# DeltaNet attention and a gelu layer on one core: row steps of the second group's inverse between decoding operations, early key norms, a back turn as copies, and U and Y out in three copies

## The chip, the cores and the metric

The kernel runs on one core of one Trainium2 chip. The metric is device time in microseconds of that core. The kernel before takes 661.88 us, the median of three runs (660.78 to 662.9). The profile is that of one execution of 660.83 us, whose recorded span is 659.1 us.

## What is computed

Attention with a state that is updated at every token, and then a two-layer network on what it gives. B = 4 batches, H = 8 heads, S = 768 tokens, D = 48; the network is 384 to 2048 to 384 wide, for 3072 tokens.

```python
k_n = k / (np.linalg.norm(k, axis=-1, keepdims=True) + 1e-06)
state = np.zeros((B, H, D, D))
for t in range(S):
    y[:, :, t] = einsum('bhd,bhde->bhe', q[:, :, t], state)
    v_old = einsum('bhde,bhd->bhe', state, k_n[:, :, t])
    state += beta[:, :, t] * einsum('bhd,bhe->bhde', k_n[:, :, t], v[:, :, t] - v_old)
x = y.transpose(0, 2, 1, 3).reshape(B * S, H * D)
h = x @ w_in
out = (0.5 * h * (1 + erf(h / sqrt(2)))) @ w_out
```

q, k, v and beta arrive as 32-bit floats, w_in and w_out as 64-bit floats, which the kernel itself turns into 32-bit ones.

## The kernel before

**Tiling.** The 768 tokens of each head are cut into 12 chunks of 64. A chunk has two *units* (a = 0, 1), each with two batches, one on each half of the 128 partitions, times 8 heads. Two chunks make a *group*: chunks 0 and 1 are group 0, chunks 2 and 3 group 1. Within a chunk the recurrence is solved at once: U is the solution of a triangular system of 64 by 64 for each head and batch, whose inverse depends on keys and beta alone and so can be made ahead; the state St passes from chunk to chunk. Q, K and V of a unit are tiles with a row for each token.

**The inverse of a group.** `grams` (L375) takes the keys' products on PE (`products`, L363) and copies them out on ACT: off-diagonal blocks to G (L382), diagonal blocks of 32 to `diag` (L386 and, for the lower half, L389). `prep` (L296), `root` (L317) and `factors` (L265) make the norms and the factor of each row; `scales` (L429) spreads the factors into XM, and `flip` (L436) turns the diagonal blocks by a DVE transpose into Nu, where the systems lie along the partitions, and scales them. Then come 30 row steps, `eliminate(j)` (L441): a product into tmp (L446) and a sum into Nu (L448), each of which reads what the one before it wrote. `back` (L454) turns Nu back by three DVE transposes: x = 0 into XM (L457), x = 1 into the right half of Zf, x = 2 into its left half (both L461). `clear` (L465) zeroes the lower left block of Zf; in group 0 one of its four parts is an ACT operation (L471), the others POOL memsets (L473). Last, `join` in group 0 (L481; `join_run`, L519, in later groups) computes the block that couples the two 32-blocks: products psJ, times a factor into XM on DVE (L503), products psJ again, copies into Zf on ACT (L507).

**A chunk.** `against_state` (L591) multiplies keys and queries by the state, `subtract` (L612) makes the right-hand side W and keeps the queries' part as y, `solve` (L628) multiplies by the inverse into psU and copies it out as U: four ACT copies of 64 partitions x 192 for each unit (L643), since pairs of heads lie on exchanged partition halves in PSUM. `use` (L645) gives psY = P U, where P are the masked products of queries and keys (`queries`, L393, copied out at L403, masked at L409), and the state's addition psS; `next_state` (L667) adds that to St on DVE, `read` (L671) takes psY out as x, again in four operations (ACT copies in chunks 0 and 1, L676; DVE additions of y later, L678). `turn` (L686) transposes x through psX into xT (L700).

**The network.** For chunks 0 and 1, `fc1` (L717) has 16 parts f of 128 of the 2048 columns (psH, L723; gelu into G by ACT, L725), and `fc2` (L732) gathers psO over the 16 f (L736). From chunk 2 on, `first_layer` and `second_layer` do the second layer with seven products of half size in place of eight (psX, psY, psZ, L761). `fc1` of chunk 1 begins before chunk 0's second layer is done: its first EARLY = 8 parts (L711) are put between chunk 0's last `fc2` steps (L847).

**The weights.** The 64-bit weights come in 16 parts: 0 to 7 are w_in, 8 to 15 w_out, each good for two f (`fetch`, L199). A part is decoded by `begin` (exponent field, DVE, L218), `exponents` (ACT, L223), `mantissas` (DVE, L230 and L232) and `signed` (DVE, L237 and L238), each operation on 128x768. That makes five DVE operations and one ACT operation for each part.

**Norms of chunks 2 and 3.** `sum_of_squares` (L285) has ACT square the keys of one head and sum them along the row, 16 calls for each chunk. V of these chunks is scaled by the norms on ACT, one call for each head (`scale_head`, L330).

**What sets the order.** The *head*, from the loads to chunk 0's xT and the decoding of parts 0 to 2, is written out by hand on all engines (L871 to L956): each engine runs its instructions in the order in which the program issues them. After it comes `plan` (L973 to L1044): steps with a time each, in units of some 58 us; all are issued in the order of their times (`emit`, L858). DVE then runs them in that order (L1045). On the other engines a scheduler may still move them; `keep_in_program_order` holds single ACT operations in place, and `together` (L563) a run of PE matmuls. `late` (L962) gives back the pools of the start, among them the PSUM tiles and the staging buffers, and zeroes Kb. An instruction waits in its engine's queue for the semaphores of its inputs, and what is behind it waits too.

Of the kernel before, what the change touches and what calls it, by code (L numbers as in the profile page):

```python
# [16 lines left out]
def kernel(  # L17
# [160 lines left out]
    G = cpool.tile([128, NF, NA * 128], F32)  # L178
    St = cpool.tile([128, NA, 2, NP, D], F32)
# [41 lines left out]
    def exponents(n):  # L221
        e = halves[n][3]
        i = nc.scalar.activation(e, e, ACT.Relu, bias=lim[:, 0:1], scale=float(2 ** 23))  # L223
        if n in (3, 4):
            tc.keep_in_program_order(i)

    def mantissas(n):
        dst, lo, hi, e = halves[n]
        bits = dst.bitcast(U32)
        nc.vector.tensor_scalar(bits, hi, 0xFFFFF, 0x100000, op0=ALU.bitwise_and,  # L230
                                op1=ALU.bitwise_or)
        nc.vector.scalar_tensor_tensor(dst, lo, 2.0 ** -32, bits, ALU.mult, ALU.add)  # L232

    def signed(n):

        dst, lo, hi, e = halves.pop(n)
        nc.vector.scalar_tensor_tensor(e, hi, 0x80000000, e, ALU.bitwise_and, ALU.bitwise_or)  # L237
        nc.vector.scalar_tensor_tensor(dst, dst, 2.0 ** -20, e.bitcast(F32), ALU.mult, ALU.mult)  # L238
        after = n + (NS if n < n_in else len(slots))
        if (after < n_in) == (n < n_in):  # L240
            fetch(after)

    def decode_steps(first, last):
        def start_(n):
            begin(n)
            exponents(n)

        steps = [(0.6, start_, first), (1.5, mantissas, first)]
        for n in range(first, last):
            if n + 1 < last:  # L250
                steps += [(0.6, start_, n + 1), (1.9, signed, n), (1.5, mantissas, n + 1)]
        return steps + [(1.9, signed, last - 1)]
# [20 lines left out]
    def squares(u, n, engine=None):  # L273
# [5 lines left out]
        if engine is None:  # L279
            nc.scalar.activation(ksq, kd, ACT.Square)  # L280
        else:
            engine.tensor_tensor(ksq, kd, kd, op=ALU.mult)
        nc.vector.tensor_reduce(n, ksq, axis=AX.X, op=ALU.add)  # L283

    def sum_of_squares(u, h):  # L285

        if "both" not in ns:
            n23 = wk.tile([128, 2 * NA, H], F32, tag="n0", name="n0", bufs=1)
            ns[2], ns[3] = n23[:, 0:NA], n23[:, NA:]
            ns["both"] = n23  # L290
        if h == 0:
            u.ksq = wk.tile([128, H, D], F32, tag="ksq", name="ksq")
        tc.keep_in_program_order(nc.scalar.activation(
            u.ksq[:, h], u.Kn[:, h, 0:D], ACT.Square, accum_out=ns[u.c][:, u.a, h:h + 1]))
# [35 lines left out]
    def scale_head(u, h):  # L330
        tc.keep_in_program_order(
            nc.scalar.mul(u.V[:, h], u.V[:, h], ns[u.c][:, u.a, h:h + 1]))
# [42 lines left out]
    def grams(us):  # L375
# [7 lines left out]
        if g > 0:  # L383
# [3 lines left out]
            for p in range(2):  # L387
                lower = slice(p * C + HB, (p + 1) * C)
                put("gram", Ds[g][lower, span], Gs[g][lower, span])  # L389

    Ps = {}
# [33 lines left out]

    def eliminate_steps(g):
# [14 lines left out]
        def eliminate(j):  # L441
# [3 lines left out]
            tmp = tmp[:, 0:n * j].rearrange("q (i c) -> q i c", i=n)  # L445
            nc.vector.tensor_tensor(tmp, nu[:, j + 1:, j:j + 1].to_broadcast([128, n, j]),  # L446
                                    nu[:, j:j + 1, 0:j].to_broadcast([128, n, j]), op=ALU.mult)
            nc.vector.tensor_tensor(nu[:, j + 1:, 0:j], nu[:, j + 1:, 0:j], tmp, op=ALU.add)  # L448
# [5 lines left out]
        def back(x):  # L454
# [7 lines left out]
            if x == 2 and g > 0:  # L462
                clear(g)

        def clear(g):  # L465
                for cc in range(2):
                    for p in range(2):
                        part = Zf[g % 2][p * C + HB:(p + 1) * C,
                                         cc * NU // 2:(cc + 1) * NU // 2, 0:HB]
                        if g == cc == p == 0:  # L470
                            nc.scalar.mul(part, low[0:HB, 0:HB // 2], 0.0)  # L471
                        else:
                            nc.gpsimd.memset(part, 0.0)  # L473

        steps = [(0.3, scales), (3.0, flip)]
        steps += [(0.7, eliminate, j) for j in range(1, HB - 1)]
        steps += [(0.1, diagonal)]
        steps += [(1.9, back, x) for x in range(3)]
        return steps + [(0.0, clear, 0)] if g == 0 else steps
# [29 lines left out]
    copies = {"join": [], "gram": []}  # L509
# [81 lines left out]
    def against_state(us):  # L591

        for u in us:
# [8 lines left out]
            for x in range(2):  # L602
                for j in range(NP):
                    for r, p in QUADS:
# [3 lines left out]
                                         rhs=St[rows, u.a, p, j, :], start=True, stop=True)  # L608
        if us[0].c != 2:
# [18 lines left out]
    def solve(us, copies=(nc.scalar.copy, nc.scalar.copy)):  # L628
        psU = dn("psU")
        for u in us:  # L630
            zf = Zf[(u.c // 2) % 2]
            u.psU = quarters(psU[:, :, u.a * NP * D:(u.a + 1) * NP * D])
            for k in range(NP // 2):
                for r in range(2):
                    for p, s in SIDES:
                        h = 4 * k + 2 * s + r
                        nc.tensor.matmul(u.psU[HALF[p ^ s], p, k, r, :],  # L637
                                         lhsT=zf[HALF[p], u.t * H + h, :],
                                         rhs=u.W[HALF[p], h, :], start=True, stop=True)
        for u, copy in zip(us, copies):  # L640
            u.U = wk.tile([128, H, D], F32, tag="U", name="U")
            for p, s in SIDES:
                copy(pairs(u.U[HALF[p]], s), u.psU[HALF[p ^ s], p])  # L643

    def use(us):  # L645

        for u in us:
# [3 lines left out]
            for k in range(NP // 2):  # L651
                for r in range(2):
                    for p, s in SIDES:
                        h = 4 * k + 2 * s + r
                        nc.tensor.matmul(u.psY[HALF[p ^ s], p, k, r, :], lhsT=u.P[HALF[p], h, :],  # L655
# [4 lines left out]
    def update(u):  # L660
        if u.c < NC - 1:
            for j in range(NP):
                for r, p in QUADS:
                    nc.tensor.matmul(u.psS[HALF[r], p, j, :], lhsT=u.Kp[HALF[p], 2 * j + r, :],  # L664
# [6 lines left out]
    def read(u, copy=nc.scalar.copy):  # L671
        u.x = wk.tile([128, H, D], F32, tag="x", name="x")
        for p, s in SIDES:
            dst, src = pairs(u.x[HALF[p]], s), u.psY[HALF[p ^ s], p]
            if u.c < 2:
                copy(dst, src)  # L676
            else:
                nc.vector.tensor_tensor(dst, src, pairs(u.y[HALF[p ^ s]], s), op=ALU.add)  # L678
# [32 lines left out]
    EARLY = 8  # L711
# [126 lines left out]
    def ffn_steps(c):  # L838
# [5 lines left out]
        if c == 0:  # L844
            twos.sort(key=lambda s: s[3])
            more_ = [(1.3, fc1, 1, f) for f in range(EARLY)]
            return ones + twos[:-2 * NA] + more_[:4] + twos[-2 * NA:-NA] + more_[4:] + twos[-NA:]  # L847
# [44 lines left out]
    scales_, flip_, *rows, back0, back1, back2, clear_ = [s_[1:] for s_ in eliminate_steps(0)]  # L892
# [3 lines left out]
    ng = wk.tile([128, NA, H], F32, tag="ng", name="ng", bufs=1)  # L896
# [3 lines left out]
    for u in first:  # L900
        transposed(u, (1,))
        queries([u])
    for a in range(NA):
# [28 lines left out]
    back2[0](*back2[1:])  # L932
    for a in range(NA):
        join(0, (a,), 1)
    clear_[0](*clear_[1:])
# [26 lines left out]
    def late():  # L962
# [3 lines left out]
        for a in range(NA):  # L966
# [3 lines left out]
            for c in range(5, NC, 2):  # L970
                tiles[c, a].Kb = Kb

    plan = [at(c + 1 + 0.25 * (c == 1), c + 2 + 0.25 * (c == 0), ffn_steps(c)) for c in range(NC)]  # L973
    plan[0][:3] = at(0.97, 0.98, [s_ for s_ in ffn_steps(0)[:1]]) + at(0.986, 1.02, ffn_steps(0)[1:3])
    plan += [at(0.985, 1.26, decode_steps(3, n_in)), at(1.26, 1.65, decode_steps(n_in, NW)), at(1.66, 1.67, [(1.0, late)])]
    rows1, join1 = eliminate_steps(1), join_steps(1)
    b = range(NA, 2 * NA)
    plan += [at(1.05, 1.051, [(1.0, together, *[(update, u) for u in first[:NA]], (join, 0, b, 0))]
                + [(1.0, next_state, u) for u in first[:NA]] + [(1.0, load, 3)]),
             at(1.1, 1.101, [(1.0, together, (join, 0, b, 1))])]  # L980
    sums = [(1.0, sum_of_squares, tiles[c, a], h) for c in (2, 3) for a in range(NA) for h in range(H)]
    plan += [at(1.08, 1.5, sums), at(1.51, 1.511, [(1.0, prep, c) for c in (2, 3)]), at(1.65, 1.655, [(1.0, finish_both)]), at(2.97, 2.971, [(1.0, finish, 4)]), at(2.725, 2.726, [(1.0, queries, third)]),
             at(1.12, 1.6, state_steps(1)),
             at(1.75, 2.43, rows1[:-1]),
             at(2.66, 2.661, [(1.0, together, join1[0])]),
             at(2.662, 2.663, rows1[-1:]),
             at(2.6, 2.601, [(1.0, together, (against_state, third))]),
             at(2.71, 2.711, [(1.0, subtract, third)]),
             at(2.7, 2.701, [(1.0, together, join1[1]), (0.0, copy_out, "join", 4)]),
             at(2.75, 2.751, [(1.0, together, join1[2]), (0.0, copy_out, "join", 4)]),  # L990
# [86 lines left out]
```

## Time and profile before

| engine | busy us | share of the span | instructions |
|---|---|---|---|
| PE (matmul) | 632.3 | 96% | 8902 |
| PEld (weight load, beside PE) | 555.6 | 84% | 8902 |
| DVE | 457.0 | 69% | 941 |
| ACT | 230.9 | 35% | 625 |
| POOL | 80.9 | 12% | 82 |

The chain that ended last is 86% PE, 5% DVE, 3% DMA and 2% ACT. The costliest groups are the first layer's matmuls (L723, 1152 records, 261.2 us), its gelu (L725, 192, 73.3 us), the row steps of all groups (L446 and L448, 180 each, 61.0 and 62.4 us) and psO (L736, 128 records, 44.8 us). The mean PE clock that was granted is 0.969 of full speed.

Busy time is time in which the engine has an instruction in hand. Matmuls are pipelined, so a busy PE need not be PE at its peak, and some matmul records can be missing. In the timelines of single engines a line gives the start (us from the span's start), the duration, the engine and source line, the operation, what it writes and reads, its shape and the number of instructions in a row; brackets at the end give the idle time before it and what ended it. Source lines are those of the kernel before.

### The profile page before, as it was taken

The page shows a single profiled execution, that of the slowest core. Times are in us where ns is not written, and L with a number is a line of the kernel's source. Part 1 is how long each engine was busy: PE and PEld are TensorE (multiplying, and loading weights), DVE is VectorE, ACT ScalarE, POOL GpSimd, SP SyncE. Part 2 cuts the span into 40 slices and gives each one's busy share as a digit, 9 for nine tenths or more (in the row PEclk, how much of TensorE's full clock was granted, in tenths as well). Part 3 has the DMA queues.
Part 4 walks back from the last instruction along what each step waited for, and adds up shares of the span by engine and source line. Part 5 has one row for each costly group of instructions (what it writes and reads, how often), then busy time and mean ns, then how long its engine had stood idle before and what let it go on. Part 6 is the DMA issues. An engine that isn't in the chain of part 4 may idle for free.

```text
span 659.1 us, 20469 instructions
## 1 busy us (share of the span) xinstructions
PE 632.3 (96%) x8902; PEld 555.6 (84%) x8902; DVE 457.0 (69%) x941; ACT 230.9 (35%) x625; POOL 80.9 (12%) x82
## 2 busy tenths in 40 slices
PE   5868999999999999999999999999999999999997
PEld 4667776676689989989989989989989989989997
DVE  7999999987879855778855778855778844325022
ACT  3465665534442136132136132136132133131220
POOL 4051011104201011301011301011301010000000
PEclk9576999999999999999999999999999999999999
DMA  9885665302424223520323620212310210100101
GB/s 128 184 257 168 122 172 143 48 2 50 82 35 72 48 37 56 93 45 12 57 36 54 98 41 17 48 18 42 59 19 19 50 14 3 25 2 2 24 1 25
DMA packets 158426, 39.68 MB, mean 60 GB/s; under 512 B 150016, under 2 KB 153216, under 8 KB 158336
## 3 DMA queue, kind: packets, MB, share of 16 engines
q1 hardware_dynamic: 152464, 33.40, 26.9%
q10 hardware_dynamic: 5872, 4.97, 3.4%
q8 instruction: 70, 1.15, 0.7%
q14 instruction: 20, 0.16, 0.1%
HBM read 33.62 MB, written 4.72 MB: 58 GB/s over the span
## 4 chain that ended last, share of the span: by engine, by line
PE 86%; DVE 5%; DMA 3%; ACT 2%; issue 2%; SPq 1%; ACTq 0%; DVEq 0%
PE psH L723 35%; PE psX L761 12%; PE psY L761 12%; PE psO L736 5%; PE psZ L761 4%; PE psG L370 4%; PE psK L607 3%; PE psJ L533 2%; PE psU L637 2%; PE psY L655 2%; PE psY L664 1%; PE psT L349 1%; DMA Kp<-in_k_dram 1%; DVE w_e L237 1%; DMA w_raw<-in_moe_w_out_dram 1%
## 5 line engine op out<-in xcount | busy, mean ns | idle before, releaser
L723 PE MATMUL psH<-xT,w_in_sb 128*128 128x256 f32 x1152 | 261.2, 384 | 3.3 <-ACT G L725 2.7
L723 PEld LDWEIGHTS psH<-xT,w_in_sb 128*128 128x128 f32 x1152 | 217.9, 192 | 36.2 <-ACT G L725 4.4
L725 ACT ACTIVATE G<-psH 128x256 f32<-128x256 f32 x192 | 73.3, 383 | 180.5 <-PE psH L723 161.9
L448 DVE TENSOR_TENSOR Nu<-Nu,tmp 128x30 f32<-128x30 f32 (+9 forms) x180 | 62.4, 347 | 6.2
L446 DVE TENSOR_TENSOR tmp<-Nu 128x30 f32<-128x30 f32 (+9 forms) x180 | 61.0, 339 | 5.0
L761 PE MATMUL psX<-w_out_sb,G 128*128 128x192 f32 x320 | 55.8, 328 | 0.0
L761 PE MATMUL psY<-w_out_sb,G 128*128 128x192 f32 x304 | 54.1, 329 | 1.1
L700 ACT COPY xT<-psX 128x384 f32<-128x384 f32 x24 | 11.4, 477 | 123.6 <-PE psX L699 122.2
L761 PEld LDWEIGHTS psX<-w_out_sb,G 128*128 128x128 f32 x320 | 52.4, 190 | 0.6
L761 PEld LDWEIGHTS psY<-w_out_sb,G 128*128 128x128 f32 x304 | 49.1, 190 | 3.3 <-DVE u L807 3.3
L308 POOL TENSOR_TENSOR n<-n,half 128x16 f32<-128x16 f32 x10 | 29.0, 2906 | 153.1 <-DVE n L283 102.8
L736 PE MATMUL psO<-w_out_sb,G 128*128 128x384 f32 x128 | 44.8, 493 | 1.4 <-DVE w_out_sb L238 1.4
L770 DVE TENSOR_TENSOR S<-G 128x512 f32<-128x512 f32 x20 | 13.8, 691 | 46.0 <-ACT G L725 45.6
L736 PEld LDWEIGHTS psO<-w_out_sb,G 128*128 128x128 f32 x128 | 23.3, 190 | 15.4 <-DVE w_out_sb L238 2.0
L620 DVE TENSOR_TENSOR W<-psK,V 128x384 f32<-128x384 f32 x22 | 12.2, 554 | 33.6 <-ACT y L619 33.6
L473 POOL MEMSET Zf<- 32x512 f32 x23 | 12.7, 554 | 166.1 <-DVE Zf L461 165.2
L643 ACT COPY U<-psU 64x192 f32<-64x192 f32 x96 | 30.0, 312 | 6.7 <-PE psU L637 5.5
L775 DVE TENSOR_TENSOR G<-G 128x512 f32<-128x512 f32 x20 | 13.8, 692 | 25.8 <-PE psX L761 25.8
L678 DVE TENSOR_TENSOR x<-psY,y 64x192 f32<-64x192 f32 x80 | 28.3, 354 | 0.9
L545 DVE TENSOR_TENSOR XM<-psJ,gm 32x256 f32<-32x256 f32 x40 | 16.8, 421 | 16.8 <-PE psJ L533 16.2
L761 PE MATMUL psY<-T,G 128*128 128x192 f32 x160 | 28.2, 329 | 0.0
L761 PE MATMUL psX<-T,G 128*128 128x192 f32 x160 | 28.1, 329 | 0.0
(141 smaller groups left out, 865.7 us busy)
## 6 DMA issues: line engine op xcount, KB each, us to landing
Kp<-in_k_dram SPq DMA_DIRECT2D x76, 96.0 KB, 3.3
w_out_sb<-in_moe_w_in_dram SPq DMA_DIRECT2D x24, 256.0 KB, 4.2
V<-in_v_dram SPq DMA_DIRECT2D x48, 96.0 KB, 3.2
out_dram<-o_sb ACTq DMA_DIRECT2D x46, 96.0 KB, 2.2
w_raw<-in_moe_w_out_dram SPq DMA_DIRECT2D x10, 384.0 KB, 5.9
Zf<-in_moe_w_out_dram SPq DMA_DIRECT2D x6, 384.0 KB, 4.1
Qp<-in_q_dram SPq DMA_DIRECT2D x64, 32.0 KB, 2.1
Qp<-in_q_dram SPq DMA_DIRECT2D x16, 96.0 KB, 4.4
```

Of the source, the lines that this page charges most:

```text
L308: nc.gpsimd.tensor_tensor(flat, flat, half, op=ALU.pow)
L370: nc.tensor.matmul(psG[HALF[p], r, i * NP + j, :], lhsT=u.Kt[rows, p, j, :], rhs=(u.Qt if x else u.Kt)[rows, p, j, :], start=True, stop=True)
L446: nc.vector.tensor_tensor(tmp, nu[:, j + 1:, j:j + 1].to_broadcast([128, n, j]), nu[:, j:j + 1, 0:j].to_broadcast([128, n, j]), op=ALU.mult)
L448: nc.vector.tensor_tensor(nu[:, j + 1:, 0:j], nu[:, j + 1:, 0:j], tmp, op=ALU.add)
L545: nc.vector.tensor_tensor(xm[low_, us, :], src, gm[low_, us].unsqueeze(2).to_broadcast([HB, H, HB]), op=ALU.mult)
L607: nc.tensor.matmul(u.psK[to, x, r, j, :], lhsT=(u.Qt if x else u.Kt)[rows, p, j, :], rhs=St[rows, u.a, p, j, :], start=True, stop=True)
L643: copy(pairs(u.U[HALF[p]], s), u.psU[HALF[p ^ s], p])
L678: nc.vector.tensor_tensor(dst, src, pairs(u.y[HALF[p ^ s]], s), op=ALU.add)
L723: nc.tensor.matmul(psH, lhsT=w_in_sb[:, f // 2, m, f % 2 * 128:(f % 2 + 1) * 128], rhs=xTs[c][:, m, :], start=(m == 0), stop=(m == NM - 1))
L725: nc.scalar.activation(G[:, f, :], psH, ACT.Gelu)
L736: nc.tensor.matmul(u.psO, lhsT=G[:, f, u.a * 128:(u.a + 1) * 128], rhs=w_out_sb[:, f, :], start=(f == 0), stop=(f == NF - 1))
L761: nc.tensor.matmul(ps_, lhsT=lhs[:, f, :], rhs=rhs[:, f, :], start=first and f == 0, stop=f == FH - 1, skip_group_check=not first)
```

## The change

It has five parts, all at the start of the kernel; later chunks are touched only by the new form of the copies and by halves of row steps.

- *Row steps between decoding operations.* `eliminate` is split in `row_product` and `row_sum`, `mantissas` and `signed` in `upper`, `lower`, `sign` and `scaled`, and the DVE order of a part is now: exponent field of the next part, sign of this one, upper of the next, scale of this one, lower of the next. Group 1's row steps, which stood behind all decoding, are spread evenly among the decoding operations of parts 8 to 15 (`alternate`). This is for DVE: dependent instructions get something between them. Chunk 0's second layer is issued two f at a time as its weights come, with chunk 1's first layer between (EARLY = 12).
- *Early norms.* The squares of chunk 2 go into the head, four behind each of chunk 0's and 1's `queries`; those of chunk 3 read the copy of the keys that `grams` uses (in Qp) and stand at 57.8 to 72 of the plan. The norms and factors then are there when the row steps are to begin.
- *Head's third back turn as copies.* The left half of Zf's upper rows equals the right half there, so `left` copies it on ACT (32x512, one for each partition half), in place of a DVE transpose; the lower left blocks are zeroed at the very start by two POOL memsets, so that `clear` is not needed in group 0. Chunk 3's two lower copies into `diag` are put behind the head's joins.
- *Three copies.* psU, psY and psS are laid out by the pair of heads and not by the partition half, so that U and x each take one operation of 128x192 and two of 64x192.
- *The plan* is written in microseconds (`on`, `once`), and ACT too keeps the written order up to `late`. Some loads and turns of chunks 4 and 5 move.

```diff
+    for p in range(2):
+        nc.gpsimd.memset(Zf[0][p * C + HB:(p + 1) * C, :, 0:HB], 0.0)
...
-        steps = [(0.6, start_, first), (1.5, mantissas, first)]
+        steps = [(0.6, start_, first), (0.6, upper, first), (0.9, lower, first)]
         for n in range(first, last):
             if n + 1 < last:
-                steps += [(0.6, start_, n + 1), (1.9, signed, n), (1.5, mantissas, n + 1)]
-        return steps + [(1.9, signed, last - 1)]
+                steps += [(0.6, start_, n + 1), (0.9, sign, n), (0.6, upper, n + 1),
+                          (1.0, scaled, n), (0.9, lower, n + 1)]
+        return steps + [(0.9, sign, last - 1), (1.0, scaled, last - 1)]
...
+        kn = u.Kn if u.c == 2 else Qp[2 + u.a]
+        nc.scalar.activation(u.ksq[:, h], kn[:, h, 0:D], ACT.Square,
+                             accum_out=ns[u.c][:, u.a, h:h + 1])
...
-                put("gram", Ds[g][lower, span], Gs[g][lower, span])
+                if us[0].c == 3:
+                    put_off("diag", Ds[g][lower, span], Gs[g][lower, span])
+                else:
+                    put("gram", Ds[g][lower, span], Gs[g][lower, span])
...
+    def left(g, ts):
+        us = slice(ts[0] * H, (ts[-1] + 1) * H)
+        for p in range(2):
+            top = slice(p * C, p * C + HB)
+            nc.scalar.copy(Zf[g % 2][top, us, 0:HB], Zf[g % 2][top, us, HB:C])
...
-            for p, s in SIDES:
-                copy(pairs(u.U[HALF[p]], s), u.psU[HALF[p ^ s], p])
+            copy(pairs(u.U, 0), u.psU[:, 0])
+            for p in range(2):
+                copy(pairs(u.U[HALF[p]], 1), u.psU[HALF[1 - p], 1])
...
-    EARLY = 8
+    EARLY = 12
...
         queries([u])
+        for h in range(4 * u.t, 4 * u.t + 4):
+            sum_of_squares(tiles[2, h // H], h % H)
...
-    back2[0](*back2[1:])
+    left(0, range(NA))
     for a in range(NA):
         join(0, (a,), 1)
-    clear_[0](*clear_[1:])
+    for step in copies.pop("diag"):
+        nc.scalar.copy(*step)
...
+    plan += [on(57.8, 72.0, [(1.0, sum_of_squares, tiles[3, a], h)
+                             for a in range(NA) for h in range(H)]),
+             once(73.0, (load, 3), (prep, 2), (prep, 3))]
...
+             on(76.8, 81.0, decode[ends[4]:ends[5]]), once(81.1, (finish_both,), *[s_[1:] for s_ in rows1[:2]]),
+             on(84.2, 125.8, alternate(decode[ends[5]:], rows1[2:-3])), once(128.6, (late,))]
+    for i in range(NF // 2):
+        t = 89.7 + 5.2 * i
+        plan += [on(t, t + 2.5, [(1.0, fc2, u, 2 * i, 2 * i + 2) for u in zero])]
+        if i < EARLY // 2:
+            plan += [fc1s(1, 2 * i, 2, t + 2.6, t + 5.1)]
...
+    with tc.manual_schedule(engines={mybir.EngineType.DVE, mybir.EngineType.Activation}):
+        emit(steps[:n])
     with tc.manual_schedule(engines={mybir.EngineType.DVE}):
-        emit(*plan)
+        emit(steps[n:])
```

## The prediction

> **What bounds the kernel now.** I read the windows by stage first, then the tensor engine's timeline, then the scalar engine's queue in the head, then the vector engine's timeline. The windows (core time, then PE, PEld, DVE, ACT and POOL busy, PE clock, DMA) show where time can be lost or won at all.
>
> ```profile
> 55.00:60.00 5.00, 4.32 (x11) 3.30 (x12) 4.90 (x7) 2.34 (x5) 0.00 (x0) 0.50 0.86 301
> 65.00:70.00 5.00, 5.00 (x113) 4.28 (x107) 4.35 (x8) 2.17 (x8) 0.00 (x0) 1.00 0.90 235
> 300.00:400.00 100.00, 99.75 (x1518) 91.40 (x1509) 71.50 (x156) 32.15 (x83) 13.20 (x11) 1.00 0.31 49
> ```
>
> From 200 us on PE is full at full clock and every other engine has slack; the built programs have the same PE order there. So the time moves only with the moment at which chunk 2's first layer starts. The PE timeline gives the marks up to it.
>
> ```profile
> 41.56 1.20 PE L492 MATMUL psJ<-XM,G 32*32 32x32 f32 x64
> 47.71 2.03 PE L637 MATMUL psU<-W,Zf 64*64 64x48 f32 x64 [1.67 <-issue]
> 56.59 6.73 PE L723 MATMUL psH<-xT,w_in_sb 128*128 128x256 f32 x18 [0.57 <-ACT xT L700]
> ...
> 100.58 2.20 PE L736 MATMUL psO<-w_out_sb,G 128*128 128x384 f32 x6 [1.37 <-DVE w_out_sb L238]
> 127.51 2.75 PE L723 MATMUL psH<-xT,w_in_sb 128*128 128x256 f32 x12
> ```
>
> The head ends at 56.59, chunk 0's second layer is done at 127.51, and chunk 2 starts at 173.33 (same view). Gaps between rows add up to some 5.5 us after 56.59; the first row runs at half clock (6.73 us for 18 records where 24 take 5.18 later). The head's ACT queue:
>
> ```profile
> 22.63 0.59 ACT L403 COPY P<-psG 128x512 f32<-128x512 f32 x1 [1.25 <-PE psG L370]
> 23.65 0.58 ACT L350 COPY Qt<-psT 128x512 f32<-128x512 f32 x1 [0.43 <-PE psT L349]
> 25.48 0.59 ACT L403 COPY P<-psG 128x512 f32<-128x512 f32 x1 [1.25 <-PE psG L370]
> ```
>
> ACT and PE alternate here with ACT's waits of 0.43 and 1.25 us. The loads of chunk 2's keys, which the change reads in this place, by the source line:
>
> ```profile
> L96 SPq DMA_DIRECT2D Kp<-in_k_dram x4: 609/900/1084, 18.7 to 21.3; - x4
> DMA to landing us min/median/max: 6.5/6.8/7.0
> ```
>
> Narrower windows give the first two issues (18.74 and 19.4) landings after 6.8 and 7.0: 26.4 us. On the vector engine:
>
> ```profile
> 59.19 0.96 DVE L238 SCALAR_TENSOR_TENSOR w_in_sb<-w_in_sb,w_e 128x768 f32<-128x768 f32 x1
> 60.06 0.55 DVE L218 TENSOR_SCALAR w_e<-w_out_sb 128x768 uint32<-128x768 uint32 x1
> 60.53 0.55 DVE L230 TENSOR_SCALAR w_in_sb<-w_out_sb 128x768 uint32<-128x768 uint32 x1
> 61.12 0.96 DVE L232 SCALAR_TENSOR_TENSOR w_in_sb<-w_out_sb,w_in_sb 128x768 f32<-128x768 uint32 x1
> ...
> 131.72 0.41 DVE L446 TENSOR_TENSOR tmp<-Nu 128x240 f32<-128x240 f32 x1
> 132.16 0.41 DVE L448 TENSOR_TENSOR Nu<-Nu,tmp 128x240 f32<-128x240 f32 x1
> 144.72 1.95 DVE L461 STREAM_TRANSPOSE Zf<-Nu 128x1024 f32<-128x1024 f32 x1
> ```
>
> It runs almost without a gap from 46.7 to 146.7: decoding until 116.1, then group 1's row steps (120.7 to 142.6). An instruction whose input isn't the one just ahead starts before that one ends (0.87 after a 0.96); one that reads it starts 0.04 after its end (0.59 after 0.55). The difference is 0.12 us.
>
> **What the Trainium skill says.** *VectorE: DVE Perf Modes*, "The DRAIN you can't avoid": the next operation doesn't start until the pipe is empty, and waits add nothing. The starts above differ: independent neighbours overlap by 0.085 us. I use the trace. *Advanced Engine Details and Errata*, "Sequencer Loop": an engine's instruction waits in its queue for its semaphores; the trace agrees where ACT's square at 178.22 waits 1.72 us for a load and the gelu ready behind it goes only at 178.65. *TensorE: Matmul & The Clock Gate*, "What's actually happening": half clock until a free-running window of about 3.4 us has been busy. The windows agree: 0.50 before 60, 1.00 after 65. *ScalarE: Activation LUTs*, "What ACT_TABLE_LOAD costs": 186 ns + 0.833 ns an element, so 0.35 us for 192 columns; the trace has 0.31 on 64 partitions, and 0.62 against 0.59 for 512 columns on 32 and 128, so partitions don't count.
>
> **The change, part by part.**
>
> *Early norms.* The 16 squares of chunk 2 now stand in ACT's hand-made order, four behind each of the four P copies. The first needs the keys of chunk 2, landed at 26.4, and ACT reaches it at 23.2. Behind it waits Qt of the next unit, for that PE's products, and behind those everything PE does in the head. Four squares take 4 x 0.23 = 0.9, so Qt starts at 27.3, not 23.65 (+3.65). From there each round is square 0.9, Qt 0.6, products 1.1, P copy 0.65: 3.3 against 2.85. After two more rounds and the last squares the copies of chunk 2's keys start at 37.3, not 32.2 (+5.1). The rest is as before: chunk 3's products end at 46.4, and psJ, behind them in PE's queue, starts there, not at 41.56. Two POOL memsets ahead of POOL's own square (about 0.9 each: 0.95 for 128x1024) delay DVE's norms and its factor XM by 1 us to 42.2; psJ's delay hides that.
>
> *Back turn as copies, diagonal copies late.* psJ's two halves at half clock end at 47.5 and 48.5, XM's four products at 49.4, the second psJ at 50.6. The two `left` copies (1.2) fit before; the join copies end at 51.35. The DVE turn (1.93) and the zeroing (0.63) are gone from this path. But ACT now has two diagonal copies (1.24) and two exponents (1.75) before it reads psU: 54.4, where before it was 49.80. psU itself, ready at 52.7, isn't the limit.
>
> *Three copies.* U and x take 6 x 0.32 each instead of 8: about 1.3 off the path. From the first U copy to the first layer was 6.8 and becomes 5.6: 60.0 against 56.59. **Head: +3.4.** In the steady part ACT and DVE wait for PE, so it is worth nothing there. State halves renamed, the halved row-step entries of later groups: nothing, PE full.
>
> *DVE.* Decoding is queued behind XM: 49.4, not 46.73. Parts 0 and 1 take 8.5 (9.5 before, with POOL's memsets beside). Part 2's exponent stands behind xT on ACT: 59.95 + 0.9, DVE waits 1 us, done 62.7. The decoding order now puts another operation between dependent ones: .47 + .88 + .47 + .88 + .88 = 3.58 a part, not 3.80. Up to part 8's mantissa: 1.94 + 5 x 3.58 + XM, state and W 4.6 + 0.2 = 24.6, so 87.3; norms, flip and scaling 4.6 (116.1 to 120.7 before): 91.9. Part 9 begins, 92.4. Only then can ACT do its exponent (0.9), which stands ahead of the x copies of chunk 1; DVE's state additions wait for those (94.3 and 95.3), and PE, whose 16 first layers end about 92, waits for x as well. Part 8 is done at 97.7, PE's second layer starts (92.59 before). Left for parts 9 to 15: decoding 6 x 3.58 + 2.6 = 24.1, and the remaining row steps 16.6 (all 60 sum to 20.0; 37 save .085, 23 still follow their own input, +.035; 1.1 is done). So 138.4. PE alone would need 5.2 for each of six rounds, two psO and one pair of first layers; DVE needs about 5.8, so DVE sets it. The last psO ends at 141.0, not 127.5.
>
> *The tail.* EARLY = 12 leaves four first layers fewer behind it. Before, 127.5 to 173.3 is 45.8; less four first layers (5.2) and gaps (1.3) is 39.3. So 180.3, +7.0. The stall of 0.9 at 178 to 179.5, ACT's square before Qt, should go, since chunk 5's keys are loaded earlier: +6.1. 661.9 + 6.1 = 668.0. V's scaling on ACT (0.28 each) and the loads moved lie beside PE.
>
> **Rivals.** (a) The keys land before ACT asks, or ACT's lag is absorbed: the head is level, all marks 3.4 earlier, 664.6. Against it: 23.2 and 26.4 above. (b) Faster: DVE starts decoding at 44.95, where the removed turn stood, never waits for ACT and overlaps nearly throughout: its sum to part 15 is 85.2 (16 parts x 3.58 = 57.3; row steps 20.0 - 3.1 + 0.8 = 17.7; norms, flip, scaling 4.6; W 2.15, XM 1.4, state 2.05), so 130.2; the last psO 132.8, chunk 2 at 172.1 less 0.9, that is 659.8, and 657 if the 23 dependent steps cost nothing either. For it: DVE has work in hand all the time. Against: the three waits named. (c) The steps overlap no better in the mix: 7 us more on DVE, 675. For it: the skill's sentence. Against: the starts above.
>
> **How the numbers follow.** Main case 0.55 at 668.0; (a) 0.15; (b) 0.20; (c) 0.10. The range reaches from (b)'s upper end, 659.8, to 672.5, two thirds of the way to (c); most of (b), 0.12, and most of (c), 0.08, are left out. Within 0.3% is 659.9 to 663.9: a third of (a) and a little of (b), 0.07. Faster is the rest of (b), 0.18. Slower 0.75.
>
> **What would show it.** ACT waiting for the key load at 23 us; psJ near 46, the first layer near 60, decoding begun near 49; 3.6 between two parts and .33 to .36 for a row step; the x copies of chunk 1 behind an exponent; PE waiting for w_out near 98 and 130 to 138; chunk 2 near 180. If the first layer starts before 57.5, the head's step is wrong; if part 15 is decoded before 132, DVE's is.

## The result, and the profile after

The changed kernel takes 669.73 us (median of four runs, 667.93 to 669.84); the kernel before took 661.33 in the runs beside it (660.73 to 662.9). The ratio is 1.0117, with a 95% interval from 1.0091 to 1.0143: slower by 8.4 us, where 668.0 and the range 659.8 to 672.5 had been given. The profiled execution is the quickest of the four (667.93), which matters for the head below. Its span is 666.2 us, 7.1 more than before.

The windows of the changed kernel (columns as before):

```profile
55.00:60.00 5.00, 4.25 (x19) 2.90 (x15) 4.41 (x7) 2.88 (x7) 1.06 (x1) 0.50 0.87 295
65.00:70.00 5.00, 5.00 (x142) 4.32 (x141) 4.50 (x8) 3.56 (x16) 0.00 (x0) 1.00 0.96 228
300.00:400.00 100.00, 99.76 (x1459) 91.34 (x1458) 69.39 (x152) 30.45 (x77) 13.17 (x11) 1.00 0.31 50
```

PE is as full from 300 to 400 as before (99.76 of 100; 99.75 before). DVE and ACT are each about 2 us less busy there, 71.50 to 69.39 and 32.15 to 30.45, with 4 and 6 instructions fewer: the three copies in place of four, which save nothing because neither engine sets the pace. The whole loss lies before chunk 2's first layer. PE's timeline (start, duration, line, what is written and read, idle time before it in brackets):

```profile
44.81 1.20 PE L531 MATMUL psJ<-XM,G 32*32 32x32 f32 x64
57.76 6.09 PE L763 MATMUL psH<-xT,w_in_sb 128*128 128x256 f32 x18 [0.57 <-ACT xT L740]
...
114.26 2.85 PE L776 MATMUL psO<-w_out_sb,G 128*128 128x384 f32 x8 [0.96 <-DVE w_out_sb L246]
...
132.91 7.12 PE L776 MATMUL psO<-w_out_sb,G 128*128 128x384 f32 x16 [2.34 <-DVE w_out_sb L246]
139.86 2.75 PE L763 MATMUL psH<-xT,w_in_sb 128*128 128x256 f32 x12
143.74 2.86 PE L763 MATMUL psH<-xT,w_in_sb 128*128 128x256 f32 x12 [1.13 <-ACT G L765]
...
180.90 4.05 PE L763 MATMUL psH<-xT,w_in_sb 128*128 128x256 f32 x18
```

Four marks are to be read: psJ 3.25 later than before, the first layer 1.2 later, the work behind chunk 0's last psO at 139.86 (127.51 before), chunk 2 at 180.90 (173.33). The brackets name w_out as what PE waits for, and the run of 16 psO that before took 5.32 us takes 7.12. In the kernel before, DVE's last step of part 15 and PE's first of chunk 2 are these:

```profile
115.23 0.96 DVE L238 SCALAR_TENSOR_TENSOR w_out_sb<-w_out_sb,w_e 128x768 f32<-128x768 f32 x1
...
173.33 4.05 PE L723 MATMUL psH<-xT,w_in_sb 128*128 128x256 f32 x18
```

The ACT timeline of the head, and DVE's in the mixed stretch, both of the changed kernel:

```profile
23.94 0.59 ACT L434 COPY P<-psG 128x512 f32<-128x512 f32 x1 [1.25 <-PE psG L397]
25.24 0.24 ACT L319 ACTIVATE ksq<-Kp 128x48 f32<-128x48 f32 x1 [0.71 <-DMA Kp<-in_k_dram]
...
26.16 0.56 ACT L377 COPY Qt<-psT 128x512 f32<-128x512 f32 x1
```

```profile
114.88 0.95 DVE L234 SCALAR_TENSOR_TENSOR w_out_sb<-w_raw,w_out_sb 128x768 f32<-128x768 uint32 x1
115.75 0.40 DVE L497 TENSOR_TENSOR Nu<-Nu,tmp 128x240 f32<-128x240 f32 x1
116.07 0.55 DVE L220 TENSOR_SCALAR w_e<-w_raw 128x768 uint32<-128x768 uint32 x1
116.54 0.40 DVE L492 TENSOR_TENSOR tmp<-Nu 128x238 f32<-128x238 f32 x1
116.97 0.41 DVE L497 TENSOR_TENSOR Nu<-Nu,tmp 128x238 f32<-128x238 f32 x1
...
135.42 0.95 DVE L246 SCALAR_TENSOR_TENSOR w_out_sb<-w_out_sb,w_e 128x768 f32<-128x768 f32 x1
136.57 2.07 DVE L506 STREAM_TRANSPOSE XM<-Nu 128x1024 f32<-128x1024 f32 x1
```

ACT waits 0.71 us for chunk 2's keys with Qt behind it. On DVE an independent neighbour starts 0.08 before the one ahead ends (115.75, 116.07, 116.54) and a dependent one 0.03 after it (116.97), so the mix gains what it was made for; but part 15 is decoded at 136.37 instead of 116.19.

| mark, us | before | forecast | after |
|---|---|---|---|
| Qt behind the first squares | 23.65 | 27.3 | 26.16 |
| psJ of group 0 | 41.56 | 46.4 | 44.81 |
| decoding begins | 46.73 | 49.4 | 47.33 |
| first layer begins | 56.59 | 60.0 | 57.76 |
| second layer of chunk 0 begins | 92.59 | 97.7 | 95.99 |
| part 15 decoded | 116.19 | 138.4 | 136.37 |
| work behind chunk 0's last psO begins | 127.51 | 141.0 | 139.86 |
| chunk 2 begins | 173.33 | 180.3 | 180.90 |

### The profile page after: what moved, and what is told of

It is laid out like the page before. It is cut to its first block, busy times and chain, and to the rows that moved or that the text cites. A ratio compares the mean times of both kernels' runs of the same rounds, so it can differ in the third digit from the quotient of the medians.

```text
span 666.2 us, 20430 instructions
## 1 busy us (share of the span) xinstructions
PE 633.7 (95%) x8902; PEld 555.5 (83%) x8902; DVE 441.3 (66%) x920; ACT 223.7 (34%) x600; POOL 82.3 (12%) x81
## 4 chain that ended last, share of the span: by engine, by line
PE 78%; DVE 9%; DMA 4%; SPq 3%; ACT 2%; issue 1%; POOL 1%; ACTq 0%; POOLq 0%
PE psH L763 33%; PE psX L801 12%; PE psY L801 12%; PE psZ L801 4%; PE psK L645 3%; PE psG L397 3%; PE psO L776 3%; PE psJ L571 2%; SPq L96 2%; PE psY L694 2%; PE psU L675 2%; DMA w_out_sb<-in_moe_w_in_dram 2%; DMA Kp<-in_k_dram 1%; SPq L212 1%; DVE Nu L497 1%
## 5 line engine op out<-in xcount | busy, mean ns | idle before, releaser
L776 PE MATMUL psO<-w_out_sb,G 128*128 128x384 f32 x128 | 46.5, 511 | 5.0 <-DVE w_out_sb L246 4.3
L334 POOL TENSOR_TENSOR n<-n,half 128x16 f32<-128x16 f32 x10 | 30.9, 3086 | 127.2 <-DVE n L308 105.0
L810 DVE TENSOR_TENSOR S<-G 128x512 f32<-128x512 f32 x20 | 13.8, 691 | 46.5 <-ACT G L765 46.1
L460 POOL MEMSET Zf<- 32x512 f32 x20 | 10.4, 518 | 194.7 <-DVE Zf L510 128.7
L801 PE MATMUL psZ<-T,S 128*128 128x192 f32 x160 | 28.1, 329 | 0.0
L362 POOL TENSOR_TENSOR V<-V,n 128x384 f32<-128x384 f32 x18 | 16.1, 905 | 84.7 <-DMA V<-in_v_dram 64.0
L801 PEld LDWEIGHTS psZ<-T,S 128*128 128x128 f32 x160 | 26.1, 190 | 0.3
```

The source lines that it names most:

```text
L334: nc.gpsimd.tensor_tensor(flat, flat, half, op=ALU.pow)
L362: engine.tensor_tensor(u.V, u.V, ns[u.c][:, u.a].unsqueeze(2).to_broadcast([128, H, D]), op=ALU.mult)
L776: nc.tensor.matmul(u.psO, lhsT=G[:, f, u.a * 128:(u.a + 1) * 128], rhs=w_out_sb[:, f, :], start=(f == 0), stop=(f == NF - 1))
L801: nc.tensor.matmul(ps_, lhsT=lhs[:, f, :], rhs=rhs[:, f, :], start=first and f == 0, stop=f == FH - 1, skip_group_check=not first)
L810: nc.vector.tensor_tensor(W2["S"][:, fs], a21, a22, op=ALU.add)
```

## The experiments

The times of the kernel before beside these runs had medians from 660.96 to 661.34. Ratios are to that kernel. What a run takes off the changed kernel is the difference of two medians. The changed kernel has four runs and an interval of 0.26% to either side, some 1.7 us; where the interval of an experiment overlaps with its 1.0091 to 1.0143, the size of the difference is uncertain by nearly as much, and the marks in the traces have to carry the argument.

**Row steps behind the decoding.** One edit of the changed kernel:

```diff
-             on(84.2, 125.8, alternate(decode[ends[5]:], rows1[2:-3])), once(128.6, (late,))]
+             on(84.2, 108.0, decode[ends[5]:]), on(108.0, 125.8, rows1[2:-3]), once(128.6, (late,))]
```

> The changed kernel with group 1's row steps behind the decoding of all parts again; everything else as changed. Theory (the row steps between the decoding operations make the w_out parts late, and PE waits for them): part 15 is decoded near 118 instead of 136, PE runs chunk 0's second layer at its own pace from 96 (8 rounds, 6 of them with two first layers: 36 us) to 132.5, chunk 2's first layer starts near 173.5 instead of 180.9, and the time is 662.5 (661 to 664.5). Rival 1 (the loss is in the head and in what stands in ACT's written order, the rows only fill DVE's idle time): under 1.5 us less, 668 to 670. Rival 2 (rows behind decoding end near 139 and group 1's inverse is then late): PE waits for psJ near 141, chunk 2 near 177, 665 to 667.

Measured: 666.7 us (665.53 to 667.38), ratio 1.0087 (1.0072 to 1.0102). That is 3.0 less than the changed kernel, between the theory's 662.5 and the first rival's 668, and what the second rival had named. Part 15 is done at 120.54 on DVE, and PE's timeline follows:

```profile
119.58 0.96 DVE L246 SCALAR_TENSOR_TENSOR w_out_sb<-w_out_sb,w_e 128x768 f32<-128x768 f32 x1
...
128.86 5.32 PE L776 MATMUL psO<-w_out_sb,G 128*128 128x384 f32 x16
134.02 2.75 PE L763 MATMUL psH<-xT,w_in_sb 128*128 128x256 f32 x12
...
144.64 1.15 PE L571 MATMUL psJ<-XM,G 32*64 32x64 f32 x32 [1.88 <-DVE XM L506]
145.72 4.54 PE L776 MATMUL psO<-w_out_sb,G 128*128 128x384 f32 x8
```

No psO waits for w_out any more: from the start of the second layer at 96.70 to 134.02 it takes 37.3 us where the changed kernel took 43.9. But group 1's rows now end at 142.4, PE waits 1.88 us for XM and again inside the next psO (4.54 for what takes 2.85), and from 134.02 to chunk 2 at 178.60 it is 44.6 us, where the changed kernel took 41.0. Half of what was won came back as another wait. So the first theory, that only the decoding is late, was too simple. The run also shows what the mixing is worth on DVE: from the scaled Nu to the last row step and the last part, DVE takes 50.6 us here (91.79 to 142.39) and 46.1 with all rows mixed in (90.41 to 136.47).

**Chunk 2's squares behind the head**, alone and together with the edit above:

```diff
-        for h in range(4 * u.t, 4 * u.t + 4):
-            sum_of_squares(tiles[2, h // H], h % H)
...
-    plan += [on(57.8, 72.0, [(1.0, sum_of_squares, tiles[3, a], h)
-                             for a in range(NA) for h in range(H)]),
+    plan += [on(57.8, 72.0, [(1.0, sum_of_squares, tiles[c, a], h)
+                             for c in (2, 3) for a in range(NA) for h in range(H)]),
```

> The changed kernel with chunk 2's 16 squares taken out of the head and put with chunk 3's into the plan behind the first layer's start (57.8 to 72). Theory: ACT no longer waits for the keys at 24.5 and has 16 x 0.23 = 3.6 us less before psJ, so psJ starts at DVE's pace, 42.6 instead of 44.8; first layer 55.6 instead of 57.8; decoding begins 2.2 earlier and, as DVE sets the pace up to part 15, chunk 2 starts 2.2 earlier: 667.5. Rival (the squares cost the same where they are put: between gelu and exponents they delay decoding as much): 669 to 671, part 15 decoded at 136 or later.

Measured: 667.23 us (666.6 to 667.84), ratio 1.0100 (1.0083 to 1.0117): 2.5 less by the medians, close to the expected 667.5, but with overlapping intervals; between the two profiled executions chunk 2 begins 1.3 earlier (179.59 against 180.90), where 2.2 had been expected. psJ starts at 42.40, behind a wait of 1.61 us for DVE's XM, and decoding at 45.85; the first layer only at 56.60 and not 55.6, because ACT copies the diagonals (47.80) and makes two exponents (49.07) before it reads psU at 50.86.

> Both of the two edits: rows behind the decoding and chunk 2's squares out of the head. Theory: the two effects are in different stretches and add up, 7.2 + 2.2: 660.3 (659 to 662), first layer near 55.6, last psO of chunk 0 near 131. Rival (the rows behind decoding are then the limit, ending near 137 whatever PE does): the head's 2 us are lost again in a wait for psJ of group 1, 662 to 664.

Measured: 664.63 us (664.42 to 664.79), ratio 1.0058 (1.0043 to 1.0073). The two edits add up (3.0 and 2.5 of 5.1), but the sum is far from the 660.3 expected, since PE's wait for XM is there as well, 1.91 us ahead of psJ at 142.67.

**The three copies alone**, in the kernel before. Edits as in the change: `solve`, `use`, `update`, `read` and the index of St.

> The kernel before with U and x in three operations and nothing else of the change. Theory: first layer 1.2 us earlier (55.4 instead of 56.6, four operations of 0.31 less on ACT's path), of which PE's wait for w_out at 99 to 100.6 takes most back since the decoding on DVE is not earlier: 661.0 (660.3 to 661.5). Rival (all of the head's gain arrives): 660.1; rival (the operation of 128x192 from two banks or halves costs more than two of 64x192): 661.5 or more, first layer not earlier.

Measured: 660.38 us (659.94 to 662.01, 12 runs), ratio 0.9998 (0.9989 to 1.0006): nothing that can be told apart. From psJ to the first layer it is 14.0 us instead of 15.0 (42.27 to 56.28 against 41.56 to 56.59), so the copies save 1.0 on this path, though psJ itself came 0.7 later in this execution. Behind it PE's wait for w_out grows from 1.37 to 1.78 us (at 100.23), and chunk 2 begins at 173.68, against 173.33. An operation of 128x192 takes 0.32 us like one of 64x192.

**Two thirds of the row steps mixed in**, the rest behind the decoding; alone, and with chunk 2's squares behind the head. The list that the edit divides has 61 instructions: the 30 row steps in two halves each, and the memset of the diagonal. So 38 are mixed in and 23 stand behind (the recorded text counts 57 and 19):

```diff
-             on(84.2, 125.8, alternate(decode[ends[5]:], rows1[2:-3])), once(128.6, (late,))]
+             on(84.2, 121.0, alternate(decode[ends[5]:], rows1[2:40])), on(121.0, 125.8, rows1[40:-3]), once(128.6, (late,))]
```

> The changed kernel with 38 of the 57 row-step pieces spread among the decoding of parts 8 to 15, and the other 19 behind it. Theory (DVE is the bound between 92 and 140 in whatever order, and two waits take turns: with all pieces mixed PE waits for w_out, with none it waits for group 1's XM): with two thirds, a part takes 3.54 + 0.65 x 2.2 = 5.0 us on DVE, less than PE's 5.2 for a round, so the last psO of chunk 0 ends near 132.5 to 134; the rows still end near 137, and XM is there near 139, before PE comes to psJ near 141 to 142; both waits gone, chunk 2's first layer near 174.5, time 663 (662 to 665). Rival (the waits only move by as much as the pieces, their sum is constant): between the two ends measured so far, 667 to 669.

Measured: 661.93 us (660.14 to 663.87, 20 runs), ratio 1.0010 (0.9999 to 1.0021). That is a little below the 662 to 665 expected. Moving 23 small instructions gives 7.8 us, more than taking all 61 out of the mix did. DVE's last step of part 15, and PE's timeline:

```profile
127.24 0.94 DVE L246 SCALAR_TENSOR_TENSOR w_out_sb<-w_out_sb,w_e 128x768 f32<-128x768 f32 x1
...
126.71 5.32 PE L776 MATMUL psO<-w_out_sb,G 128*128 128x384 f32 x16
131.87 2.75 PE L763 MATMUL psH<-xT,w_in_sb 128*128 128x256 f32 x12
...
140.55 1.15 PE L571 MATMUL psJ<-XM,G 32*64 32x64 f32 x32
```

Neither run of psO nor psJ has a bracket: both waits are gone. Part 15 is decoded at 128.2 and the rows still end at 136.5, as with all of them mixed. This is what a bound by DVE with two due dates looks like: PE wants part 15 near 129 and group 1's XM near 140; with all rows ahead of part 15 DVE misses the first date, with none ahead of it the second. Shares other than all, none and 38 were not run.

> The kernel with two thirds mixed, with chunk 2's squares out of the head as well. Theory: the head's 1.2 to 2.5 us come on top, 661 (660 to 663). Rival (without waits in the middle the head's gain is swallowed by one that comes back): as two thirds mixed alone, within 0.5 us.

Measured: 660.25 us (659.73 to 662.32, 12 runs), ratio 0.9988 (0.9977 to 0.9998). The head's gain comes on top, 1.7 us.

**EARLY = 16** in the changed kernel:

```diff
-    EARLY = 12
+    EARLY = 16
...
-             on(131.5, 164.0, ffn_steps(1)[4:])]
+             on(131.5, 164.0, ffn_steps(1))]
```

> The changed kernel with EARLY = 16: also the last four first layers of chunk 1 between chunk 0's last rounds of the second layer. Theory (PE stands idle for w_out between 120 and 136, DVE sets when part 15 is there): they fill idle time; last psO near 140.5 as before, four first layers (5.2 us) fewer behind it, of which 0.5 is lost: chunk 2 near 176.3 and 665 (664 to 667). Rival (PE's order is its own bound and the waits seen are the chain's own length): last psO 2.5 to 5 us later, no gain, 669 to 670.

Measured: 666.56 us (665.19 to 667.52), ratio 1.0078 (1.0056 to 1.0100): 3.2 less. PE did have idle time in which four more first layers fit; the tail behind the last psO is 37.9 us (141.54 to 179.46). Its head is the changed kernel's, in an execution in which the keys landed later:

```profile
26.34 0.24 ACT L319 ACTIVATE ksq<-Kp 128x48 f32<-128x48 f32 x1 [2.40 <-DMA Kp<-in_k_dram]
```

```profile
46.39 1.92 PE L531 MATMUL psJ<-XM,G 32*32 32x32 f32 x64
...
60.03 8.31 PE L763 MATMUL psH<-xT,w_in_sb 128*128 128x256 f32 x24 [0.57 <-ACT xT L740]
```

Four of the profiled kernels have the changed kernel's head unaltered. The first squares start at 25.24, 25.47, 26.25 and 26.34, psJ at 44.81, 44.15, 45.46 and 46.39, the first layer at 57.76, 57.50, 59.12 and 60.03 (changed, two thirds, rows behind, EARLY 16). The two heads with late keys are the two late ones, but landing alone does not place them: it differs by 1.1 us and the first layer by 2.5, and the earliest keys don't give the earliest head. From the first square to psJ it is 18.7 to 20.1 us, with the same products of PE taking different times (the last 64 of psG ahead of psJ 1.18 us in two thirds, 1.99 in EARLY 16). Whether late keys made the three other executions of the changed kernel longer than the profiled one is not shown: they have no profile.

**The keys' loads first.**

```diff
     load_v(0)
+    load_k(2, "Kp")
     for n in range(2):
         fetch(n)
-    load_k(2, "Kp")
```

> The changed kernel with chunk 2's key loads issued ahead of the first two weight parts instead of behind them. Theory (the squares cost the head in two ways: ACT waits for the keys, 0.7 to 2.7 us in the runs so far, and then 16 x 0.23 us of squares stand in its queue): the wait is gone, the squares stay; Qt follows the first four squares at once, psJ near 43.7 to 44 in every execution, first layer near 57.3, and the time falls to 667.5 (666.5 to 668.5), the changed kernel's fastest run. Rival (the squares alone are the cost): 669.5 or more, psJ near 46. Second rival (weights part 0 lands later and decoding begins later): DVE begins after 48 and 670 or more.

Measured: 666.81 us (665.91 to 667.3), ratio 1.0086 (1.0070 to 1.0102): 2.9 less than the changed kernel by the medians. The squares stand where the change put them and start at 24.45 without a wait; psJ follows at 43.15, the first layer at 56.66, decoding at 45.96. That is all that moving the squares out had brought (667.23). So it is mostly the wait for the keys that costs, and little the squares' own 16 x 0.23 us: with the squares gone PE waits for DVE's XM instead, and psJ starts only 0.75 earlier (42.40).

**The back turn as a DVE transpose again**: `back2` in place of `left`, the clearing behind the joins, no early memsets.

```diff
-    left(0, range(NA))
+    back2[0](*back2[1:])
     for a in range(NA):
         join(0, (a,), 1)
+    clear(0)
```

> The changed kernel with the head's third back turn as a DVE transpose again, and the lower left blocks zeroed behind it as in the kernel before; no copies of the left half, no early memsets. Theory (psJ comes late because of ACT's queue, so the turn lies beside it in the head, but DVE begins to decode later by its length and DVE sets the pace up to part 15): first layer within 0.5 us of the changed kernel's, decoding begins 1.9 later, part 15 at 138.3, chunk 2 near 182.8, 671.5 (670.5 to 672.5). Rival (the copies on ACT cost the head as much as the turn costs DVE): 669 to 670.

Measured: 670.13 us (669.01 to 672.29), ratio 1.0137 (1.0112 to 1.0163), against the changed kernel's 1.0117 (1.0091 to 1.0143). The times don't tell the two apart, and the 671.5 expected was not reached. The marks lean to the theory: beside the EARLY 16 profile, whose keys landed at the same moment (26.42 and 26.34), decoding begins at 51.13 instead of 49.28 and part 15 is done at 140.41 instead of 138.72, 1.7 to 1.9 later. What the copies are worth in time stays open between 0 and 2 us.

**Three waits at once.** On the kernel with two thirds mixed and norms behind the head: diagonal copies behind xT, Kb zeroed by POOL, chunk 5's squares issued later.

```diff
-            nc.scalar.mul(Kb.rearrange("q p j h n -> q (p j h n)"),
-                          low.rearrange("q a b -> q (a b)")[:, 0:NP * 4 * HB], 0.0)
+            nc.gpsimd.memset(Kb.rearrange("q p j h n -> q (p j h n)"), 0.0)
```

> The kernel with two thirds mixed and the norms behind the head, and three edits to waits seen in the trace: chunk 3's two lower diagonal copies go behind chunk 0's xT copies on ACT (1.25 us ahead of U's copies before), Kb is zeroed by POOL instead of ACT (ACT reached the gelus 1.12 us late), and chunk 5's squares are issued after chunk 2's xT (ACT waited for their keys, and psX for xT, 1.8 us). Theory (PE is the bound now, so each wait taken from it counts whole): 1.2 + 1.1 + 1.8 = 4.1 less than 660.25: 656.2 (655.5 to 658). Rival (DVE, whose XM is there at 138, is the bound again as soon as PE is 2 us earlier): 658 to 659, a new wait of PE for psJ near 137.

Measured: 661.11 us (660.3 to 661.57), ratio 0.9998 (0.9990 to 1.0006): nothing won. Each of the three had been read wrongly. The diagonal copies moved behind xT (56.20) push part 2's exponent back, and the second layer begins at 96.21 instead of 95.19. The gelus still came 1.16 us late, because ACT issues chunk 0's four output transfers just ahead of them. And chunk 5's squares did not move: the plan's time orders DVE, while the scheduler put the ACT instruction back where it had been.

**The same waits, at their cause.** On the kernel with two thirds mixed and norms behind the head again, chunk 0's outputs go out by SP's queue, and the squares are held in program order and issued behind xT:

```diff
-            if u.c == 4:
+            if u.c in (4, 5):
                 tc.keep_in_program_order(i)
...
-            send(u)
+            send(u, queues=(nc.sync, nc.sync) if u.c == 0 else (nc.scalar, nc.scalar))
```

> The kernel with two thirds mixed and the norms behind the head, and two edits to ACT's queue: chunk 0's outputs are sent by SP's queue instead of ACT's (the two issues took 1.2 us each ahead of the gelus that PE waited for at 134), and chunk 5's squares are held behind chunk 2's xT copies (they waited for their keys until 158.6 and 160.6 with xT and PE's psX behind them; in the combined kernel they stayed where they were). Theory (PE has no other wait left between 57 and 180, so both count whole): 1.1 + 1.8 less than 660.25: 657.4 (656.5 to 658.5). Rival (something else on ACT's or SP's queue then ends last, as in the combined kernel): 660 to 661.

Measured: 658.77 us (658.26 to 659.13), ratio 0.9966 (0.9954 to 0.9978), faster than the kernel before and than the changed one. It is 1.5 less than 660.25, half of the 2.9 expected, and just outside the range given. The output issues were the cause of the gelus' lateness:

```profile
132.07 5.34 PE L763 MATMUL psH<-xT,w_in_sb 128*128 128x256 f32 x24
```

The last four first layers run in one piece. The squares' wait left behind 0.37 of its 1.8 us. Some of it came back: DVE's XM (L583) now ends two waits of PE, 0.30 and 0.67 us at 143.6 and 144.6. That is the rival of the expectation before this one, on a small scale.

## Why the prediction was right, and where not

- **Which stretch counts.** Right. From chunk 2's start to the end it is 485.8 us before and 485.3 after: 7.6 us are lost ahead of it and 0.5 won behind it, 7.1 in the span. The stall at 178 to 179.5 had been taken to give 0.9. The forecast's difference was 6.1; it is 7.1 between the two profiled executions and 8.4 between the medians.
- **Early norms.** The mechanism is right: ACT waits for the keys and PE's head waits behind ACT. In the profiled execution the size was off, +1.2 instead of +3.4 at the first layer. Half of the 2.2 us between them is the landing of the keys (25.2, not 26.4); the rest lies behind it, from Qt to psJ (18.65 us, 19.1 worked out) and from psJ to the first layer (12.95, 13.6 worked out). With keys at 26.34 the same head gave 46.39 and 60.03, the forecast's 46.4 and 60.0. The forecast took one execution's landing, and one pace of PE, for constants. Loading the keys first took 2.9 us off. XM's delay lay beside psJ's, as forecast, but it ends a path once the squares are gone: with the norms behind the head psJ waits for it (1.61 us). What part the two memsets on POOL have in it was not measured: XM's transpose starts at 40.16 there, and at 39.21 and 39.99 in two profiles of the head without them.
- **Diagonal copies and exponents ahead of psU on ACT.** Right in part as to which of them ends last. In the kernel with norms behind the head PE finishes psU at 49.65 and ACT reads it at 50.86. In the changed kernel's own profile the two end together, ACT's exponents at 51.92 and psU at 51.98, and with two thirds mixed ACT waits 0.50 us for psU: there it does not hold that psU isn't the limit.
- **Three copies.** Worth 1.0 us in the head, 1.3 forecast, and nothing in the steady part, as forecast. That the kernel before gains nothing from them, because PE then waits longer for w_out, had not been part of the forecast's sum.
- **DVE sets the pace.** Right, and the main term: from part 8 done (95.89) to part 15 done (136.37) it is 40.5 us, and 40.7 had been worked out. The order without dependent neighbours takes 3.54 us for a part (start to start, 72.36 to 75.90), 3.58 forecast. Rival (c), no overlap, is excluded by these starts. It rested on half of what the Trainium skill says: *VectorE: DVE Perf Modes*, "The DRAIN you can't avoid", goes on that an operation which is not held starts earlier. In this trace independent neighbours do, by 0.08 us. The x copies of chunk 1 did stand behind part 9's exponent (DVE idle 0.76 and 0.44 us), as said.
- **Which part of the mix costs.** Here the forecast was silent and the runs add something: the loss is not the mixing but its amount. Putting a third of the rows behind gave 7.8 us, putting all of them there 3.0.
- **The tail.** The one step of wrong size: 39.3 us were worked out from the last psO to chunk 2, 41.0 were measured. The four first layers (5.2) were right; the gaps of 1.3 that should go were replaced by 1.13 (gelus behind output issues) and 1.57 (psX behind chunk 5's squares; the changed kernel's bracket names DVE's gm, and ACT's xT for the same wait in other profiles, 1.78 us with two thirds mixed). These are more than the error: the work between the waits took about 1 us less than worked out. With both taken away at their cause it is 39.8 (132.07 to 171.85). That error and the smaller head nearly cancelled in the profiled execution, 180.90 against 180.3. So its 667.93, next to the forecast of 668.0, is partly luck; the median is 1.7 above it.
- **Rivals.** (a), a level head, fell with the key wait; (b), no wait for ACT on DVE, with the three waits, all of which are in the trace: 1.14 us for psJ ahead of XM, 0.48 for part 2's exponent, 0.76 and 0.44 for the x copies.

Together: putting a third of the row steps behind the last weight part takes 7.8 us off the changed kernel, and taking chunk 2's squares out of the head then 1.7 more. These 9.5 are more than the 8.4 lost, and what is left of the change, with both mended, is a ratio of 0.9988 (0.9977 to 0.9998).

## What to carry to other kernels

When one engine prepares things for another, list each product with its due date and put work in between only as far as the next date allows: here 38 instructions in the gap left no wait on either side, and 61 and none each left one. An instruction that waits for a load must not stand in a hand-ordered queue ahead of one on which the critical engine depends; look up when the load lands, in more than one execution. And before a wait is mended, look at what the waited-for engine did just before: the nearest instruction is not always the cause, as output issues hidden in ACT's queue showed.

## What was not expected of the hardware

The same load of chunk 2's keys, at the same place in the program and begun at 18.5 to 19.2 us, landed between 25.2 and 26.4 us in different executions. Behind it, in a hand-ordered queue, the first layer's start spread over 2.5 us (57.5 to 60.0); part of that is PE's pace. The 64 products of psJ in the head took 1.20 us in some profiles and 1.92 in others, and the clock column of the windows doesn't tell which: it shows 1.00 from 45 to 50 us in the profile of EARLY = 16, where they took 1.92. The ends of matmuls are modelled in such a profile, but DVE, which reads the products, bears it out: its first product from psJ begins 0.74 us after psJ's start in the changed kernel's profile (45.55) and 1.11 us after it in that of EARLY = 16 (47.50).
